# Decode attention with gated output: V read by whole batches through one ring of five 32 KB buffers

## The chip, the cores and the metric

One NeuronCore of a Trainium2 chip runs the whole kernel. The metric is the device time of one execution in microseconds. Engines are named as in the profile: PE (matmul), DVE, ACT, POOL, and SP, which only issues transfers here. A core has 16 DMA engines, and every large transfer is spread over all of them.

## The reference

One decode step for 8 sequences (batches): layer norm of `x`, attention over the last 2048 of 8192 cached positions with 32 query heads on 8 cached heads of 128, and a gated branch that multiplies the attention's result.

```python
# x: (8, 1, 512)   k_cache, v_cache: (8, 8, 8192, 128)   wq: (512, 4096)   wo: (4096, 512)
xn = layernorm(x)
W = min(4096, max(256, Sk // 4))                    # 2048
q = (xn @ wq).reshape(B, 1, 32, 128).transpose(0, 2, 1, 3)
k = repeat(k_cache[:, :, Sk - W:, :], 4, axis=1)    # 4 query heads share a cached head
v = repeat(v_cache[:, :, Sk - W:, :], 4, axis=1)
p = softmax(einsum("bhqd,bhkd->bhqk", q, k) * 128 ** -0.5)
s = (einsum("bhqk,bhkd->bhqd", p, v)).transpose(0, 2, 1, 3).reshape(B, 1, 4096) @ wo
h = sigmoid(xn @ w_gate) * (xn @ w_up)              # 512 x 1792 each
g = silu(h @ w_down)                                # 1792 x 512
return x + s * g
```

All inputs are bf16. The windows of K and of V are 33.5 MB each, `wq` and `wo` 4.2 MB each, the gated branch's weights 1.8 MB each: 81 MB are read.

## The kernel before

**Staging.** Everything is read once, all large reads by SP, in one order written out in `loads`: `wq`, K tiles 0 to 6, V tiles 0 and 1, K tile 7, V tiles 2 to 13, `w_gate` and `w_up`, V tiles 14 and 15, `w_down`, and `wo` in six pieces of 16, 8, 4, 2, 1 and 1 of its 32 rows per partition. There are two rings of buffers. `kring` has 3 of 32 KB per partition and takes `wq`, the K tiles and the three other weights; `vring` has 4 of 16 KB per partition and takes the V tiles. `issue_loads` puts the next load of the list on SP's queue once the tile that had its buffer before, 3 or 4 places back in the same ring, is in `released`, and it never passes one load over for a later one. In the program that comes out, SP's instruction waits for the reader of that older tile, so the loads behind it on SP wait too.

**Slots.** The loop over `t` writes the engines' orders by hand, one slot at a time. In slot `t` DVE turns an eighth of a K tile (`k_turn`, L464); four slots later PE multiplies it with the queries (`qk`, L479). K has 8 tiles of 8 slots, in two sets (`hb`) of four batches. At `EXP_AT[hb]` a set's softmax starts: `soft_exp` on ACT (L507), `soft_turn` on DVE (L527), `soft_spread` (PE L540, ACT L548), which brings the probabilities to the partitions of V, `soft_den` for the denominators. `soft_mask` (L561) multiplies them on DVE with the head masks `Hm`, so that one matmul can serve several heads whose rows stand in one contraction. From slot `PV_LAG` = 52 on PE takes V (`pv`, L609), beside the last K slots at first.

**V.** A V tile is half a batch: 4 of 8 cached heads, 32 runs of 64 positions by 4 heads on the 128 partitions, 16 KB each. `pv` makes 16 matmuls of a tile in 4 slots; each has a weight of 64 columns (4 heads x 4 position chunks x 4 query heads) and 512 columns of V (4 chunks x 128), and two of them fill the two halves of the output's 128 rows (`tile_position`). After the fourth slot ACT copies the sum to SBUF (L623). `pv_sum` (L635), once for four tiles and at the end for 2, 1 and 1, picks the diagonal blocks out of it with f32 matmuls against `Sel`, and DVE applies 1/denominator (L644).

**End.** `unit_in` (L355) and `unit_mid` make the gated branch's hidden layer once its weights are in, after V tile 13. After the last V tile `o_rows` (L657, DVE L664) brings the heads to the rows of `wo`, `unit_out` (L381) does `w_down`, and 64 matmuls (L723, 2 per row of `wo`) follow the pieces of `wo` as they land. DVE multiplies by the gate (L734), adds `x` (L736), and two transfers write the output.

The lines that tie loads to buffers:

```python
order, n = (v_order, VRING) if kind == 1 else (k_order, KRING)
at = order.index(x)
if at >= n and order[at - n] not in released:
    break
```

Of the kernel before, what the change touches and what calls it, by code (L numbers as in the profile page):

```python
# [10 lines left out]
def kernel(  # L11
# [13 lines left out]
    nc = tc.nc  # L25
# [18 lines left out]
    PP = P // GL  # L44
    CH = W // PP
    NQ = P // 32
    NJ = 4
    CC = CH // NJ
    NT = B * NG
# [11 lines left out]
    VSET = NT // HB  # L61
# [14 lines left out]
    NCH = 4  # L76
    KRING = 3
    VRING = 4
    CG = CH // NCH
# [17 lines left out]
    kring = ctx.enter_context(tc.tile_pool(name="kring", bufs=KRING))  # L97
    vring = ctx.enter_context(tc.tile_pool(name="vring", bufs=VRING))
# [19 lines left out]
    def k_tile(shape, name):  # L118
        return kring.tile(shape, bf16, name=name, tag="kring", align_bytes=ALIGN)

    def v_tile(shape, name):
        return vring.tile(shape, bf16, name=name, tag="vring", align_bytes=ALIGN)
# [8 lines left out]
    wq_sb = k_tile([P, KT, Hq * Dh], "wq_sb")  # L131
# [8 lines left out]
    def load_k(i):  # L140
        hb, kq = divmod(i, NK)
        t = k_tile([P, KC, Dh], "k_sb")
# [9 lines left out]
    def v_of(i):  # L152
        hb, n = divmod(i, VSET)
        gg, q = divmod(n, NQ)
        return NQ * hb + q, gg
# [15 lines left out]
    def load_gate_up():  # L171
        t = k_tile([P, 2, KT, F], "wgu_sb")
        for n, w in enumerate((B_w_gate, B_w_up)):
            load(t[:, n], w.rearrange("(p kt) n -> p kt n", kt=KT))
            wgu_sb.append(t[:, n])

    def load_down():
        t = k_tile([P, FT, D], "wd_sb")
# [6 lines left out]
    def load_wo():  # L185
        t = k_tile([P, KW, D], "wo_sb")
# [56 lines left out]
    x_f = ppool.tile([B, D], f32, name="x_f", tag="pp")  # L243
    nc.vector.tensor_copy(out=x_f[:], in_=x_bf[:])  # L244
    stats = work.tile([B, nc.vector.BN_STATS_DIM], f32, name="stats")
    nc.vector.bn_stats(out=stats[:], in_=x_f[:])
    mv = work.tile([B, nc.vector.BN_AGGR_DIM], f32, name="mv")
    nc.vector.bn_aggr(out=mv[:], in_=stats[:])
    eps_t = work.tile([B, 1], f32, name="eps_t")
    nc.vector.memset(eps_t[:], 1e-5)  # L250
    rstd = work.tile([B, 1], f32, name="rstd")
# [19 lines left out]
    for c in range(NCOL):  # L271
# [32 lines left out]
    Hm = consts.tile([P, GL], f32, name="Hm")  # L304
    nc.vector.tensor_reduce(
        out=Hm[:],
        in_=ident[:].rearrange("p (a gl) -> p gl a", gl=GL),
# [3 lines left out]

    spread = consts.tile([P, NG, 2, PP, GL], bf16, name="spread")
    nc.gpsimd.memset(spread[:].rearrange("p a b c d -> p (a b c d)").bitcast(f32), 0.0)
    for j in range(GL):
        for gg in range(NG):
            g = NG * gg + j // 2
            nc.gpsimd.tensor_copy(
                out=spread[:, gg, j % 2, :, j], in_=ident[:, 32 * g : 32 * g + PP]
            )

    w = NCH * GL * rep
    rows_of = ppool.tile([P, w], f32, name="rows_of", tag="pp")
    nc.vector.tensor_reduce(
        out=rows_of[:],
        in_=ident[:].rearrange("p (a m) -> p m a", m=w),
        axis=AX.X,
        op=ALU.add,
    )
    Sel = consts.tile([P, NCH, GL, rep], f32, name="Sel")
    nc.vector.tensor_copy(  # L330
        out=Sel[:], in_=rows_of[:].rearrange("p (g c r) -> p c g r", g=GL, c=NCH)
# [3 lines left out]
    pick = consts.tile([32 * NG, NE, P], bf16, name="pick")  # L335
    nc.gpsimd.memset(pick[:].rearrange("p e m -> p (e m)").bitcast(f32), 0.0)
    for gg in range(NG):
        rows = slice(32 * gg, 32 * (gg + 1))
        cols = slice(NE * GL * rep * gg, NE * GL * rep * (gg + 1))
        for e in range(NE):  # L340
            nc.gpsimd.tensor_copy(
                out=pick[rows, e, cols].rearrange("p (h d) -> p h d", d=NE)[:, :, e],
                in_=ident[rows, 32 * gg : 32 * gg + GL * rep],
            )
# [108 lines left out]
    o_sb = work.tile([32 * NG, B, Dh], bf16, name="o_sb")  # L453
    nc.vector.memzero(o_sb[:])
# [76 lines left out]
    def soft_spread(hb):  # L531

        pt = pt_of.pop(hb)[:].rearrange("p c (y m) -> p c y m", y=2)
        pc = ppool.tile([P, NG, NQ, CH, rep], bf16, name="pc_bf", tag="pp")
        for gg in range(NG):
            for ch in range(2):
                c = slice(CB * ch, CB * (ch + 1))
                pT_ps = psum_a.tile([P, CB, NQ, rep], f32, name="pT_ps", tag="acc_ps")
                for y in range(2):
                    nc.tensor.matmul(  # L540
                        pT_ps[:],
                        lhsT=spread[:, gg, y].rearrange("p k g -> p (k g)"),
# [4 lines left out]
                    )  # L547
                nc.scalar.copy(  # L548
                    out=pc[:, gg, :, c, :].rearrange("p q c r -> p c q r"),
# [4 lines left out]
    def soft_mask(hb, gg):  # L554

        pT_of[hb, gg] = work2.tile(
            [P, NQ * CG, GL, NCH * rep], bf16, name="pT_sb"
        )
        pc = pc_of[hb][:, gg].rearrange("p q (c e) r -> p (q c) (e r)", e=NCH)
        for gl in range(GL):  # L560
            nc.vector.tensor_scalar(  # L561
                out=pT_of[hb, gg][:, :, gl, :],
                in0=pc,
                scalar1=Hm[:, gl : gl + 1],
# [3 lines left out]

    GW = GL * rep

    def soft_den(hb):
# [8 lines left out]
        den_ps = psum1.tile([32 * NG, NQ], f32, name="den_ps", tag="misc")  # L580
        rden = small.tile([32 * NG, NQ], f32, name="rden")
        for gg in range(NG):
            rows = slice(32 * gg, 32 * gg + GW)
            nc.tensor.matmul(  # L584
                den_ps[rows, :],
                lhsT=HR[:, GL * gg : GL * (gg + 1)].rearrange("m h r -> m (h r)"),
                rhs=dq[:],
                start=True,
                stop=True,
                tile_position=(0, 32 * gg),  # L590
                skip_group_check=True,
            )
            nc.vector.reciprocal(out=rden[rows, :], in_=den_ps[rows, :])
        rden_of[hb] = rden

    def pv(t):


        i, j = divmod(t, NJ)
        b, gg = v_of(i)  # L600
        w = GL * rep * NCH
        if j == 0:
            acc_tiles[i] = psum_a.tile([P, NCH * Dh], f32, name="acc_ps", tag="acc_ps")
        q = b % NQ
        pT = pT_of[b // NQ, gg][:, CG * q : CG * (q + 1)].rearrange("p c g n -> p (c g n)")
        for n in range(CC // NCH):
            c = n % (P // w)
            ch = CC * j + NCH * n
            nc.tensor.matmul(  # L609
                acc_tiles[i][w * c : w * (c + 1), :],  # L610
                lhsT=pT[:, GL * rep * ch : GL * rep * ch + w],
                rhs=v_tiles[i][:, ch : ch + NCH, :].rearrange("p c d -> p (c d)"),
                start=(j == 0 and n < P // w),
                stop=(j == NJ - 1 and n >= CC // NCH - P // w),
                tile_position=(0, w * c),
                skip_group_check=True,
            )
        if j == NJ - 1:
            if i % NSUM == 0:
                acc_sbs[i // NSUM] = work.tile(  # L620
# [3 lines left out]
                out=acc_sbs[i // NSUM][:, i % NSUM], in_=acc_tiles.pop(i)[:]  # L624
            )

    def pv_sum(i, n):

        b, gg = v_of(i)
        q = b % NQ  # L630
        acc_sb = acc_sbs[i // NSUM][:, i % NSUM : i % NSUM + n]
        rows = slice(32 * gg, 32 * gg + GW)
        o_ps = psum1.tile([32 * NG, NSUM, Dh], f32, name="o_ps", tag="misc")
        for c in range(NCH):
            nc.tensor.matmul(  # L635
                o_ps[rows, :n, :],
                lhsT=Sel[:, c].rearrange("p g r -> p (g r)"),
# [3 lines left out]
                tile_position=(0, 32 * gg),  # L641
# [3 lines left out]
            out=o_sb[rows, b : b + n, :],  # L645
            in0=o_ps[rows, :n, :],
            in1=rden_of[b // NQ][rows, q : q + n].unsqueeze(2).to_broadcast([GW, n, Dh]),
# [21 lines left out]
    for t in range(PV_LAG + NSLOT):  # L669
# [3 lines left out]
        for hb in range(HB):  # L673
            if t == EXP_AT[hb]:
                soft_exp(hb)
            for gg in range(NG):
                if t == MASK_AT[hb, gg]:
                    soft_mask(hb, gg)
# [9 lines left out]
        if u >= NJ and u % NJ == 0:  # L688
            i = u // NJ - 1
            if i == NT - 2:  # L690
                pv_sum(i, 1)
# [80 lines left out]
```

## Time and profile before

| | |
|---|---|
| median of 3 runs | 197.33 us (197.1 to 197.42) |
| profiled execution, its own time | 197.29 us |
| its span in the profile | 195.5 us |
| PE busy | 102.9 us (53%), 750 instructions |
| DVE busy | 105.5 us (54%), 149 |
| ACT busy | 30.8 us (16%), 69 |
| SP's data queue (q1) | 81.01 MB, 97.0% of the 16 engines' span |
| mean granted PE clock | 0.903 |

The span runs from the first to the last instruction that the profiler recorded; the profiled execution took 1.8 us more than that. A chain of waits is followed back from the last instruction. In the tables of windows, each column gives an engine's busy microseconds and its instructions in brackets, then the granted clock, the share of the 16 DMA engines, and GB/s. Times in the text such as "at 173.1" are microseconds from the start of the span.

### The profile page before, as it was taken

The numbers are of one execution on the slowest core, as the hardware profiler recorded it, in microseconds if no ns is written. First come the engines' busy times: TensorE is split into PE (matmuls) and PEld (weight loads), VectorE is DVE, ScalarE is ACT, GpSimd is POOL, SyncE is SP. The second block draws the span as 40 slices with busy tenths as digits, with TensorE's granted clock in tenths as the row PEclk, the third lists the DMA queues.
The fourth block names the chain that finished last, engine by engine and source line by source line (L and its number), as shares of the span: only waits on it lengthen the run. The fifth ranks groups of instructions, "written<-read, shape, count | busy, mean of one in ns | idle before, by whom it ended". The sixth has DMA issues, their size and how long they took to land.

```text
span 195.5 us, 1888 instructions
## 1 busy us (share of the span) xinstructions
PE 102.9 (53%) x750; PEld 36.2 (19%) x750; DVE 105.5 (54%) x149; ACT 30.8 (16%) x69; POOL 4.6 (2%) x25
## 2 busy tenths in 40 slices
PE   0062014434323258403695989858944893577763
PEld 0020001101000012100121222322311131223551
DVE  0156499999899998899969726403100010040301
ACT  2025050000000084000011143511111114010100
POOL 8000000000000000000000000000000000000000
PEclk9999999999999999955588799988999798597999
DMA  7999999999999999999999999999999999999990
GB/s 276 423 476 429 436 429 429 429 429 421 429 429 429 429 429 429 389 432 463 429 419 432 436 422 429 427 429 429 429 429 432 429 431 425 431 429 432 425 390 30
DMA packets 5128, 81.14 MB, mean 415 GB/s; under 512 B 616, under 2 KB 896, under 8 KB 1152
## 3 DMA queue, kind: packets, MB, share of 16 engines
q1 hardware_dynamic: 5056, 81.01, 97.0%
q8 instruction: 6, 0.10, 0.2%
q10 hardware_dynamic: 64, 0.01, 0.0%
q14 instruction: 2, 0.02, 0.0%
HBM read 81.01 MB, written 0.01 MB: 414 GB/s over the span
## 4 chain that ended last, share of the span: by engine, by line
DMA 62%; DVE 23%; PE 10%; issue 1%; ACT 1%; SPq 0%; DVEq 0%
DMA k_sb<-in_A_k_cache_dram 31%; DMA v_sb<-in_A_v_cache_dram 22%; DVE k_sb L464 18%; DMA wo_sb<-in_A_wo_dram 10%; PE acc_ps L609 4%; DVE pt_bf L527 2%; PE s_ps L479 2%; PE pT_ps L540 2%; PE o_ps L635 2%; DVE mx L493 1%; SPq L116 0%; DVE qz_sb L434 0%; DVE o_sb L644 0%; PE den_ps L584 0%; DVE qT_sb L424 0%
## 5 line engine op out<-in xcount | busy, mean ns | idle before, releaser
L464 DVE STREAM_TRANSPOSE k_sb<-k_sb 128x1024 f32<-128x1024 f32 x64 | 73.7, 1210 | 6.7 <-DMA k_sb<-in_A_k_cache_dram 6.6
L479 PE MATMUL s_ps<-k_sb,qz_sb 128*32 128x512 bf16 x256 | 29.8, 565 | 54.2 <-DVE k_sb L464 48.4
L609 PE MATMUL acc_ps<-v_sb,pT_sb 128*64 128x512 bf16 x256 | 39.6, 443 | 10.7 <-DMA v_sb<-in_A_v_cache_dram 10.6
L644 DVE TENSOR_TENSOR o_sb<-o_ps,rden 16x512 bf16<-16x512 f32 (+2 forms) x6 | 3.0, 504 | 47.5 <-PE o_ps L635 47.5
L479 PEld LDWEIGHTS <-qz_sb 128*32 128x32 bf16 x256 | 8.5, 116 | 78.6 <-issue 55.3
L623 ACT COPY acc_sb<-acc_ps 128x512 f32<-128x512 f32 x16 | 9.4, 586 | 84.7 <-PE acc_ps L609 84.7
L609 PEld LDWEIGHTS <-pT_sb 128*64 128x64 bf16 x256 | 13.3, 120 | 31.5 <-DMA v_sb<-in_A_v_cache_dram 14.6
L635 PE MATMUL o_ps<-acc_sb,Sel 128*16 128x512 f32 (+2 forms) x48 | 15.9, 477 | 3.4 <-ACT acc_sb L623 3.4
L561 DVE TENSOR_SCALAR pT_sb<-pc_bf,Hm 128x1024 bf16<-128x1024 bf16 x16 | 6.6, 477 | 6.7 <-PE acc_ps L609 6.7
L507 ACT ACT_TABLE_LOAD x1 | 1.3, 1283 | 39.9 <-DVE nm L501 39.9
L635 PEld LDWEIGHTS o_ps<-acc_sb,Sel 128*16 128x16 f32 x48 | 4.5, 103 | 14.9 <-issue 7.7
L493 DVE TENSOR_REDUCE mx<-s_ps 128x1 f32<-128x512 f32 x8 | 5.3, 662 | 3.2 <-PE s_ps L479 3.2
L540 PE MATMUL pT_ps<-pt_bf,spread 128*128 128x512 bf16 x16 | 6.0, 501 | 1.3 <-DVE pt_bf L527 0.7
L267 PE MATMUL xnT_ps<-ident,xn_bf 8*128 8x8 bf16 x4 | 0.3, 174 | 11.6 <-DVE xn_bf L257 11.6
L436 ACT COPY qz_sb<-qT_sb 32x32 bf16<-32x32 bf16 x20 | 4.8, 241 | 8.2 <-DVE qT_sb L424 7.9
L355 PE MATMUL d_ps<-wgu_sb,xnT_sb 128*32 128x448 bf16 x32 | 3.0, 511 | 5.3 <-DMA wgu_sb<-in_B_w_up_dram 3.0
L723 PE MATMUL a_ps<-wo_sb,o_sb 128*32 128x256 bf16 x64 | 4.5, 273 | 2.0 <-DMA wo_sb<-in_A_wo_dram 2.0
L507 ACT ACTIVATE p_bf<-s_ps,nm 128x512 bf16<-128x512 f32 x8 | 5.4, 686 | 0.0
L244 DVE CAST x_f<-x_bf 8x512 f32<-8x512 bf16 x1 | 0.4, 415 | 9.2 <-DMA x_bf<-in_A_x_dram 9.2
L548 ACT CAST pc_bf<-pT_ps 128x512 bf16<-128x512 f32 x8 | 4.5, 587 | 5.0 <-DVE pt_bf L527 2.8
L527 DVE STREAM_TRANSPOSE pt_bf<-p_bf 128x512 bf16<-128x512 bf16 x8 | 4.9, 668 | 0.0
L723 PEld LDWEIGHTS <-o_sb 128*32 128x32 bf16 x64 | 3.5, 96 | 3.1 <-issue 3.0
(59 smaller groups left out, 39.4 us busy)
## 6 DMA issues: line engine op xcount, KB each, us to landing
k_sb<-in_A_k_cache_dram SPq DMA_DIRECT2D x8, 4096.0 KB, 19.3
v_sb<-in_A_v_cache_dram SPq DMA_DIRECT2D x16, 2048.0 KB, 15.7
wq_sb<-in_A_wq_dram SPq DMA_DIRECT2D x1, 3072.0 KB, 11.4
wo_sb<-in_A_wo_dram SPq DMA_DIRECT2D x1, 2048.0 KB
wgu_sb<-in_B_w_gate_dram SPq DMA_DIRECT2D x1, 1792.0 KB
wgu_sb<-in_B_w_up_dram SPq DMA_DIRECT2D x1, 1792.0 KB, 24.7
wd_sb<-in_B_w_down_dram SPq DMA_DIRECT2D x1, 1792.0 KB
wq_sb<-in_A_wq_dram SPq DMA_DIRECT2D x1, 1024.0 KB, 4.6
```

Of the source, the lines that this page charges most:

```text
L436: nc.scalar.copy(out=out, in_=in_)
L464: nc.vector.transpose(out=kw, in_=kw)
L479: nc.tensor.matmul(s_tiles[i][32 * g : 32 * (g + 1), :], lhsT=qz_sb[:, hb, h, 2 * a + e, :], rhs=kT[:, :, a, h, :, e], start=(n == 0), sto ...
L493: nc.vector.reduce_max(out=mx_of[hb][:, kq : kq + 1], in_=s_tiles[i][:], axis=AX.X)
L507: nc.scalar.activation(out=p_bf[:, :, kq], in_=s_tiles.pop(NK * hb + kq)[:].rearrange("p (o c j) -> p c j o", o=2, j=NC), func=AF.Exp, bia ...
L527: nc.vector.transpose(out=pt[:, w * n : w * (n + 1)], in_=p_bf[:, w * n : w * (n + 1)])
L540: nc.tensor.matmul(pT_ps[:], lhsT=spread[:, gg, y].rearrange("p k g -> p (k g)"), rhs=pt[:, c, y, :], start=(y == 0), stop=(y == 1), skip_ ...
L561: nc.vector.tensor_scalar(out=pT_of[hb, gg][:, :, gl, :], in0=pc, scalar1=Hm[:, gl : gl + 1], scalar2=None, op0=ALU.mult,)
L609: nc.tensor.matmul(acc_tiles[i][w * c : w * (c + 1), :], lhsT=pT[:, GL * rep * ch : GL * rep * ch + w], rhs=v_tiles[i][:, ch : ch + NCH, : ...
L623: nc.scalar.copy(out=acc_sbs[i // NSUM][:, i % NSUM], in_=acc_tiles.pop(i)[:])
L635: nc.tensor.matmul(o_ps[rows, :n, :], lhsT=Sel[:, c].rearrange("p g r -> p (g r)"), rhs=acc_sb[:, :, Dh * c : Dh * (c + 1)], start=(c == 0 ...
L723: nc.tensor.matmul(a_ps[32 * c : 32 * (c + 1), :], lhsT=o2_sb[:, k, :], rhs=wo_parts[k][:, DC * c : DC * (c + 1)], start=(k == 0), stop=(k ...
```

## The change

A V tile becomes a whole batch: 8 heads by 16 runs of 128 positions, 32 KB per partition, in one transfer; the last batch's comes in two halves of 16 KB. The two rings become one of five buffers of 32 KB (160 KB per partition, as the two rings had together), in the one order of `loads`, so a load waits for the tile five places back, whatever it holds. `w_gate` and `w_up` stand ahead of the last V tile. `pv` has 32 matmuls per tile in 8 slots, each with a weight of 128 columns (8 heads x 4 chunks x 4 query heads), no longer two side by side. Masks are made per batch, 8 of 512 elements per partition for batch `b` at `MASK_AT[b]`; those of batches 0 and 1 in the same slots as before, that of batch `b` later with the start of tile `b - 1`'s products (`pT_sb` still has two buffers). `pv_sum` comes for 4, 3 and 1 batches, and its outputs, the denominators and `pick` use 32 rows in place of two groups of 16. `wo` is cut into pieces of 12, 9, 5, 3, 2 and 1. Three small tiles of the layer norm share one, and `x` comes in two transfers instead of three.

```diff
-    NJ = 4
-    CC = CH // NJ
-    NT = B * NG
+    RUNS = P // Hkv
+    CV = W // RUNS
+    NCH = 4
+    CG = CV // NCH
+    NJ = 8
+    CGJ = CG // NJ
+    NT = B
...
-    MASK_AT = {}
-    for gg in range(NG):
-        MASK_AT[0, gg] = EXP_AT[0] + 9 + gg
-        MASK_AT[1, gg] = max(EXP_AT[1] + 6, PV_LAG + NJ * NQ * (gg + 1))
+    MASK_AT = {0: EXP_AT[0] + 9, 1: EXP_AT[0] + 10}
+    for b in range(2, NT):
+        MASK_AT[b] = PV_LAG + NJ * (b - 1)
...
-    KRING = 3
-    VRING = 4
+    RING = 5
...
-    for c0, c1 in ((0, 2), (2, 3), (3, 4)):
+    for c0, c1 in ((0, 2), (2, 4)):
         nc.scalar.dma_start(
...
-    def load_v(i):
-        b, gg = v_of(i)
-        t = v_tile([P, CH, Dh], "v_sb")
-        load(
-            t[:].rearrange("p c d -> p (c d)"),
-            A_v_cache[b, GL * gg : GL * (gg + 1), win0:Sk, :].rearrange(
-                "j (p c) d -> p j (c d)", c=CH
-            ),
-        )
-        v_tiles[i] = t
+    v_runs = A_v_cache[:, :, win0:Sk, :].rearrange(
+        "b h (k c) d -> b k h (c d)", c=CV
+    )
+
+    def load_v(b):
+        t = big([P, CV, Dh], "v_sb")
+        flat = t[:].rearrange("p c d -> p (c d)")
+        parts = 2 if b == NT - 1 else 1
+        n = CV * Dh // parts
+        for h in range(parts):
+            load(flat[:, n * h : n * (h + 1)], v_runs[b, :, :, n * h : n * (h + 1)])
+        v_tiles[b] = t
...
-            (0, 16),
-            (16, 24),
-            (24, 28),
-            (28, 30),
-            (30, 31),
+            (0, 12),
+            (12, 21),
+            (21, 26),
+            (26, 29),
+            (29, 31),
             (31, 32),
...
-    loads[-2:-2] = [(2, 0)]
+    loads[-1:-1] = [(2, 0)]
     loads = loads + [(2, 1), (2, 2)]
-    k_order = [(4, 0)] + [x for x in loads if x[0] != 1]
-    v_order = [x for x in loads if x[0] == 1]
+    order = [(4, 0)] + loads
...
-            order, n = (v_order, VRING) if kind == 1 else (k_order, KRING)
-            at = order.index(x)
-            if at >= n and order[at - n] not in released:
+            at = loads_done[0] + 1
+            if at >= RING and order[at - RING] not in released:
                 break
...
+    def soft_mask(b):
+
+        pT_of[b] = work2.tile([P, CG, Hkv, NCH * rep], bf16, name="pT_sb")
+        pc = pc_of[b // NQ][:, b % NQ].rearrange("p (c e) r -> p c (e r)", e=NCH)
+        for h in range(Hkv):
             nc.vector.tensor_scalar(
-                out=pT_of[hb, gg][:, :, gl, :],
+                out=pT_of[b][:, :, h, :],
                 in0=pc,
-                scalar1=Hm[:, gl : gl + 1],
+                scalar1=Hm[:, h : h + 1],
...
+    def pv(t):
+
+
+        b, j = divmod(t, NJ)
+        if j == 0:
+            acc_tiles[b] = psum_a.tile([P, NCH * Dh], f32, name="acc_ps", tag="acc_ps")
+        for cg in range(CGJ * j, CGJ * (j + 1)):
             nc.tensor.matmul(
+                acc_tiles[b][:],
+                lhsT=pT_of[b][:, cg].rearrange("p h n -> p (h n)"),
+                rhs=v_tiles[b][:, NCH * cg : NCH * (cg + 1), :].rearrange(
+                    "p c d -> p (c d)"
+                ),
+                start=(cg == 0),
+                stop=(cg == CG - 1),
                 skip_group_check=True,
             )
...
+        if u == NJ * NSUM:
+            pv_sum(0, NSUM)
+        elif u == NSLOT - NJ // 2:
+            pv_sum(NSUM, NT - NSUM - 1)
...
-        if u == NSLOT - 2 * NJ - 1:
+        if u == NSLOT - NJ - 1:
             unit_in(wgu_sb[0])
             unit_in(wgu_sb[1])
             released.add((2, 0))
             issue_loads()
-        if u == NSLOT - 2 * NJ:
+        if u == NSLOT - NJ:
             unit_mid()
```

More of the change, by code (lines that the diff above doesn't have):

```diff
@@ L60 @@
     SET = NK * KTS
-    VSET = NT // HB
     QK_LAG = 4
@@ L116, in load, with big @@
         q.dma_start(out=dst, in_=src)
[L118 to L122, printed above, removed]
+    def big(shape, name):
+        return ring.tile(shape, bf16, name=name, tag="ring", align_bytes=ALIGN)
     x_bf = work.tile([B, D], bf16, name="x_bf")
-    for c0, c1 in ((0, 2), (2, 3), (3, 4)):
+    for c0, c1 in ((0, 2), (2, 4)):
         nc.scalar.dma_start(
@@ L141, in load_k @@
         hb, kq = divmod(i, NK)
-        t = k_tile([P, KC, Dh], "k_sb")
+        t = big([P, KC, Dh], "k_sb")
         k0 = win0 + NC * KC * kq
@@ L302 @@
     )
-    Hm = consts.tile([P, GL], f32, name="Hm")
+    Hm = consts.tile([P, Hkv], f32, name="Hm")
     nc.vector.tensor_reduce(
         out=Hm[:],
-        in_=ident[:].rearrange("p (a gl) -> p gl a", gl=GL),
+        in_=ident[:].rearrange("p (a h) -> p h a", h=Hkv),
         axis=AX.X,
@@ L310 @@
     )
[L312 to L316, printed above, removed]
+    spread = consts.tile([P, 2, 2, P], bf16, name="spread")
+    nc.gpsimd.memset(spread[:].rearrange("p a b c -> p (a b c)").bitcast(f32), 0.0)
+    for o in range(2):
+        for y in range(2):
             nc.gpsimd.tensor_copy(
-                out=spread[:, gg, j % 2, :, j], in_=ident[:, 32 * g : 32 * g + PP]
-            )
[L321 to L329, printed above, removed]
+                out=spread[:, o, y].rearrange("p (k g s) -> p s g k", g=NQ, s=2)[:, y],
+                in_=ident[:].rearrange("p (g k o) -> p o g k", k=RUNS, o=2)[:, o],
+            )
+    Sel = consts.tile([P, NCH, Hkv, rep], f32, name="Sel")
     nc.vector.tensor_copy(
-        out=Sel[:], in_=rows_of[:].rearrange("p (g c r) -> p c g r", g=GL, c=NCH)
+        out=Sel[:], in_=ident[:].rearrange("p (h c r) -> p c h r", c=NCH, r=rep)
     )
     NE = P // Hq
-    pick = consts.tile([32 * NG, NE, P], bf16, name="pick")
+    pick = consts.tile([Hq, NE, P], bf16, name="pick")
     nc.gpsimd.memset(pick[:].rearrange("p e m -> p (e m)").bitcast(f32), 0.0)
[L337 to L344, printed above, removed]
+    for e in range(NE):
+        nc.gpsimd.tensor_copy(
+            out=pick[:, e, :].rearrange("p (h d) -> p h d", d=NE)[:, :, e],
+            in_=ident[:Hq, :Hq],
+        )
     FQ = F // 4
@@ L452 @@
     acc_sbs = {}
-    o_sb = work.tile([32 * NG, B, Dh], bf16, name="o_sb")
-    nc.vector.memzero(o_sb[:])
+    o_sb = work.tile([Hq, B, Dh], bf16, name="o_sb")
     def k_turn(t):
@@ L533, in soft_spread @@
         pt = pt_of.pop(hb)[:].rearrange("p c (y m) -> p c y m", y=2)
-        pc = ppool.tile([P, NG, NQ, CH, rep], bf16, name="pc_bf", tag="pp")
-        for gg in range(NG):
+        pc = ppool.tile([P, NQ, CV, rep], bf16, name="pc_bf", tag="pp")
+        for o in range(2):
             for ch in range(2):
@@ L547, in soft_spread @@
                     )
+                cv = slice(CH * o + CB * ch, CH * o + CB * (ch + 1))
                 nc.scalar.copy(
-                    out=pc[:, gg, :, c, :].rearrange("p q c r -> p c q r"),
+                    out=pc[:, :, cv, :].rearrange("p q c r -> p c q r"),
                     in_=pT_ps[:],
@@ L579, in soft_den @@
         )
[L580 to L593, printed above, removed]
+        den_ps = psum1.tile([Hq, NQ], f32, name="den_ps", tag="misc")
+        rden = small.tile([Hq, NQ], f32, name="rden")
+        nc.tensor.matmul(
+            den_ps[:],
+            lhsT=HR[:].rearrange("m h r -> m (h r)"),
+            rhs=dq[:],
+            start=True,
+            stop=True,
+        )
+        nc.vector.reciprocal(out=rden[:], in_=den_ps[:])
         rden_of[hb] = rden
     def pv(t):
-        i, j = divmod(t, NJ)
-        b, gg = v_of(i)
-        w = GL * rep * NCH
+        b, j = divmod(t, NJ)
         if j == 0:
[L603 to L615, printed above, removed]
+            acc_tiles[b] = psum_a.tile([P, NCH * Dh], f32, name="acc_ps", tag="acc_ps")
+        for cg in range(CGJ * j, CGJ * (j + 1)):
+            nc.tensor.matmul(
+                acc_tiles[b][:],
[5 more added lines that the diff above has]
+                stop=(cg == CG - 1),
                 skip_group_check=True,
@@ L618, in pv @@
         if j == NJ - 1:
-            if i % NSUM == 0:
-                acc_sbs[i // NSUM] = work.tile(
+            if b % NSUM == 0:
+                acc_sbs[b // NSUM] = work.tile(
                     [P, NSUM, NCH * Dh], f32, name="acc_sb"
@@ L623, in pv, with pv_sum @@
             nc.scalar.copy(
[L624 removed]
+                out=acc_sbs[b // NSUM][:, b % NSUM], in_=acc_tiles.pop(b)[:]
             )
[L627 to L629 removed]
+    def pv_sum(b, n):
         q = b % NQ
[L631 to L633 removed]
+        acc_sb = acc_sbs[b // NSUM][:, b % NSUM : b % NSUM + n]
+        o_ps = psum1.tile([Hq, NSUM, Dh], f32, name="o_ps", tag="misc")
         for c in range(NCH):
             nc.tensor.matmul(
[L636 to L637 removed]
+                o_ps[:, :n, :],
+                lhsT=Sel[:, c].rearrange("p h r -> p (h r)"),
                 rhs=acc_sb[:, :, Dh * c : Dh * (c + 1)],
@@ L644, in pv_sum @@
         nc.vector.tensor_tensor(
-            out=o_sb[rows, b : b + n, :],
-            in0=o_ps[rows, :n, :],
-            in1=rden_of[b // NQ][rows, q : q + n].unsqueeze(2).to_broadcast([GW, n, Dh]),
+            out=o_sb[:, b : b + n, :],
+            in0=o_ps[:, :n, :],
+            in1=rden_of[b // NQ][:, q : q + n].unsqueeze(2).to_broadcast([Hq, n, Dh]),
             op=ALU.mult,
@@ L675 @@
                 soft_exp(hb)
-            for gg in range(NG):
-                if t == MASK_AT[hb, gg]:
-                    soft_mask(hb, gg)
+        for b in range(NT):
+            if t == MASK_AT[b]:
+                soft_mask(b)
         if t < KSLOT:
```

49 lines of the change are left out of this document (14 added, 35 removed).

## The prediction

> **What bounds the kernel now.** I read the slices of the page first, then the chain that ended last, then the groups, and last the timelines of PE and DVE near the end. The slices, and one window of the V stage:
>
> ```profile
> GB/s 276 423 476 429 436 429 429 429 429 421 429 429 429 429 429 429 389 432 463 429 419 432 436 422 429 427 429 429 429 429 432 429 431 425 431 429 432 425 390 30
> DMA packets 5128, 81.14 MB, mean 415 GB/s; under 512 B 616, under 2 KB 896, under 8 KB 1152
> ```
> ```profile
> 110.00:160.00 50.00, 38.27 (x226) 12.32 (x224) 10.62 (x24) 11.32 (x23) 0.00 (x0) 0.93 1.00 428
> ```
>
> After the first slice the transfers run at about 429 GB/s to the end, with K (slices 4 to 17) and with V (18 on) alike; the single dips to 389 and 419 stand beside 432 and 463 and are packets booked in the neighbouring slice. The packet records confirm it: each of the 16 DMA engines starts a packet as the one before ends. 81.0 MB at 429 GB/s are 189 us of a 195.5 us span: the kernel is as long as its reads, plus a start of 2 us and an end of 3.4 us. The chain in order of time shows that end:
>
> ```profile
> 128.32 16.83 DMA v_sb<-in_A_v_cache_dram
> ...
> 147.14 25.99 DMA v_sb<-in_A_v_cache_dram
> 173.13 0.02 issue
> 173.15 18.96 DMA wo_sb<-in_A_wo_dram
> 192.11 0.04 issue
> 192.15 0.30 PE a_ps L723 x2
> 192.45 0.02 issue
> 192.47 0.42 DVE prod L734
> 192.90 0.02 issue
> 192.92 0.28 DVE y_bf L736
> ```
>
> The last piece of wo lands at 192.11; everything else is done by then. So the change can act in three ways only: on the time a byte takes, on an issue that comes too late to keep the engines fed, or on compute that is not ready for the last wo piece.
>
> ```profile
> L464 DVE STREAM_TRANSPOSE k_sb<-k_sb 128x1024 f32<-128x1024 f32 x64 | 73.7, 1210 | 6.7 <-DMA k_sb<-in_A_k_cache_dram 6.6
> L609 PE MATMUL acc_ps<-v_sb,pT_sb 128*64 128x512 bf16 x256 | 39.6, 443 | 10.7 <-DMA v_sb<-in_A_v_cache_dram 10.6
> L561 DVE TENSOR_SCALAR pT_sb<-pc_bf,Hm 128x1024 bf16<-128x1024 bf16 x16 | 6.6, 477 | 6.7 <-PE acc_ps L609 6.7
> ```
>
> V's matmuls wait for V's transfers (10.6 us), K's transposes for K's (6.6): the engines run after the data.
>
> **Part by part. 1, packets.** The bytes and their order are unchanged; V goes from 16 transfers with 16 KB runs to 7 with 32 KB runs and two halves with 16 KB. K is read in 32 KB runs already, so both prices are in the trace: one engine needs 1.210 us from packet to packet of 32 KB, 0.6074 us of 16 KB, and about 6 ns for the semaphore write of a transfer. Per engine 4 MB of V are 16 x 0.6074 + 2 x 0.006 = 9.73 us now and 8 x 1.210 + 0.006 = 9.69 us then; landings 4.86 us apart for 2 MB and 9.68 us for 4 MB say the same. Seven tiles save 7 x 0.043 = 0.30 us. wo is cut otherwise (12, 9, 5, 3, 2, 1 of 32 for 16, 8, 4, 2, 1, 1): six pieces, as many packets, the same last piece, so nothing. One x transfer fewer is 8 packets of 18 ns beside wq, which is the later: nothing.
>
> [...]
>
> **2, one ring of five.** A load now needs the tile five places back. From a tile's landing to the moment when the load that replaces it must be queued lie four tiles, some 39 us. Dating the releases by the trace: k0 is free at 35 (SP issues k3 at 34.98), needed for k5 by 60; k3 at 64.6, needed for k7 by 89; k5 at 92, for v2 by 109; v0 at about 106, for v4 by 127; k7 at 116, for v5 by 137. Every margin is above 15 us, so SP's waits stay ahead of the engines, though the ring is in one order. No cost; without that cover an issue late by some us would cost as many.
>
> **3, V's products.** Before, two 64-column matmuls ran side by side: 16 took 1.92 us at full clock, 0.22 us a pair, and at the half clock 3.56:
>
> ```profile
> 173.18 1.92 PE L609 MATMUL acc_ps<-v_sb,pT_sb 128*64 128x512 bf16 x16 [0.76 <-DMA v_sb<-in_A_v_cache_dram]
> 178.03 3.56 PE L609 MATMUL acc_ps<-v_sb,pT_sb 128*64 128x512 bf16 x16 [1.21 <-DMA v_sb<-in_A_v_cache_dram]
> 123.34 1.08 PE L540 MATMUL pT_ps<-pt_bf,spread 128*128 128x512 bf16 x4 [0.40 <-ACT pc_bf L548]
> ```
>
> Now 256 matmuls of 128 columns stand one by one. The L540 row gives their spacing, (1.08 - 0.38) / 3 = 0.23 us, and PE's own starts 0.216; I take 0.22, so a tile of 32 needs 7.1 us, under the 9.7 that its read takes, and 13.7 at the half clock. Added PE time 256 x 0.11 = 28 us, all beside transfers. Taken out: half of the f32 sums of L635 (15.9 us to about 8) and 8 evictions of 0.59 us.
>
> **4, masks.** 64 of 512 elements for 16 of 1024 (0.40 us apart). Between a half (0.20) and a whole (0.40) I take 0.28: 18 us for 6.6. Those of batches 0 and 1 lie among K's transposes: 16 x 0.28 - 3.3 = 1.2 us late, less 0.5 for one den round trip instead of two; DVE waits 1.95 us for k7 at 101.5, so it hides. Batch 2's mask waits for V tile 0's last product and stands ahead of k7's last four transposes: PE's slots there are 0.33 + 0.86 = 1.2 us, as long as DVE's, and the second softmax comes some 1.5 us later than at 114.4. V tile 2, the first behind it, lands at 121; with the half clock for one window and L540's eight products it is done at 131.5, tile 3 at 138.6, the first sum at 142.2, tile 4 at 149.3, and tile 5 lands at 150: caught up.
>
> **5, the end.** The first half of v7 lands at 172.9, the second at 177.7. At full clock: 16 products 3.5 us to 176.4, the sum over three batches 8 x 0.32 = 2.6 to 179.0, second half to 182.6, eviction to 183.3, last sum to 184.4, o_sb 184.7, pick 185.3, cast 1.29 to 186.6, b_ps beside it; wo's 64 matmuls (3.5 us) from 186.8 could end at 190.3. Before they began at 187.12, at a landing. wo lands until 191.8, so 1.5 us are spare, and one half-clock window of 3.4 us, the length in the trace, costs 1.7. It just hides.
>
> **Sum.** 192.11 - 0.30 = 191.8, then 3.4 us as now: span 195.2; the profiled execution took 197.29, 1.79 more than its span: 196.99. The median is 0.04 higher: 197.03. A measurement of this kernel can tell about 0.2% (0.39 us) from no change; this is 0.15%.
>
> **Rivals.** *A DMA engine that loses twice.* Each of the six 16 KB packets of q8 (instructions) holds one engine up by 0.9 us and its next packet by 0.5; the 8 KB ones of q14 by 0.3 and 0.5. After the first of each at 46 to 48 us the 16 landings of a transfer lie 1.6 us apart instead of 0.3, and stay so: each fetch hits another engine, so the slowest carries one. DVE has some 40 instructions more and PE as many as now. One more fetch, or another sequence, on an engine already late costs 0.8 to 1.4 us: 197.8 to 198.4. For it: half the engines are already hit. Against: eight fetches have not met so far. 0.14.
>
> *PE late at the end, so slower.* The granted clock fell to 0.5 at 178.1 after a window with 1.5 us of work in 3.4, and at 82.6, 106.5, 130.4, 150.8, 164.5 likewise. In the new order PE is idle 3 us before v7's first half, so one cold window is likely; a second, in b_ps and wo's products, makes 3.4 - 1.5 = 1.9 us at most: 197.5 to 198.9. It decides from the point where wo's products start later than 188.3. Against: from 172.9 to 182.6 PE now has work without a pause. 0.09. [...]
>
> [...] 0.02.
>
> *Fewer transfers gain more*: if each of the 7 dropped transfers stood in the line with its own start-up, the 1.1 us from the first issue (0.74) to the first packet (1.80), 197 - 8 = 189. The back-to-back packets are against it. 0.01. [...]
>
> *The change as described, ending on the read* has the remaining 0.74. Its own range is 196.6 to 197.4: the 0.30 may be 0.1 to 0.6, since which engine is hit last moves the end by up to the 0.3 us that landings differ before any fetch, and the three runs before spread over 0.3. About 0.32 of it lies below 196.94, 0.40 within 0.2%, 0.02 above. With the rivals: faster 0.33, same 0.40, slower 0.27. The range goes up to 198.1, into the first two rivals, and down to 196.5.
>
> **What would show it.** Right: GB/s at 429 to the last slice, last wo landing near 191.8, the chain still ending in wo; 32 V matmuls in about 7 us; masks near 0.28 us each; SP issues long ahead of use. Wrong: a slice under 420 in the V stage (a late issue, or pitch), landings of one transfer 2.5 us apart (a double fetch), or PE's wo products running on after the last landing without waiting.

## The result and the profile after

The changed kernel takes 285.49 us (median of 4 runs, 282.46 to 289.29), the kernel before 197.36 (4 runs, 197.1 to 197.42): ratio 1.442, 95% interval [1.429, 1.455]. The forecast was 197.0, within 196.5 to 198.1. The profiled execution is the longest of the four, 289.29 us with a span of 287.5, so differences of two per cent or less are not read from it.

The slices of the page, and the window that answers the one of before, in the V stage (its last figure is GB/s, the one before it the share of the DMA engines):

```profile
GB/s 311 419 438 438 438 434 435 438 438 438 438 223 217 205 374 292 205 214 214 219 214 217 219 211 191 205 210 214 221 210 220 204 237 341 203 219 217 346 339 22
DMA packets 4104, 81.13 MB, mean 282 GB/s; under 512 B 480, under 2 KB 640, under 8 KB 1024
```
```profile
110.00:160.00 50.00, 22.28 (x112) 6.42 (x111) 17.69 (x34) 3.86 (x10) 0.00 (x0) 0.70 1.02 213
```

K's seven tiles still run at 438 GB/s. From the twelfth slice on, where V begins, it is about 214, half of it, at a DMA share of 1.02: the 16 engines are not waiting for an issue, each packet simply takes longer. The packet records say the same: 32 KB of K take 1.213 us, 32 KB of V mostly 2.37 to 2.55 (median 2.50). In K tile 7 (374 and 292) and the weights (341, 346, 339) the rate rises again.

The end of the chain (steps below 0.6 us left out), and V's products and the masks among the groups:

```profile
217.50 9.71 PE acc_ps L576 x32
228.04 9.57 another core or an unknown queue
237.96 3.84 another core or an unknown queue
242.14 9.02 another core or an unknown queue
251.18 32.59 DMA wo_sb<-in_A_wo_dram
283.81 0.63 PE a_ps L684 x6
```
```profile
L576 PE MATMUL acc_ps<-v_sb,pT_sb 128*128 128x512 bf16 x256 | 76.5, 458 | 76.7 <-DMA v_sb<-in_A_v_cache_dram 76.7
L540 DVE TENSOR_SCALAR pT_sb<-pc_bf,Hm 128x512 bf16<-128x512 bf16 x64 | 17.4, 343 | 50.1 <-PE acc_ps L576 50.1
```

The chain still ends in the last piece of `wo`, now at 283.8 instead of 192.1. PE waits 76.7 us for V, 10.6 before. The place of the loss is V's reading: 33.5 MB at 213 instead of 429 GB/s are 157 us instead of 78, 79 of the 92 us between the two profiled executions. The other 13 us, by subtraction, lie among K tile 7 and the weights, whose packets run in between: the 16 landings of one V transfer are 7.5 us apart (1.6 before), so fast and slow transfers are in flight together. If each engine's packets are followed by their starts and ends, K tile 7's first ones, from 99 us on, took mostly 2.2 to 2.4 us, the next mostly 1.3 to 1.5, and from 104 us on 1.21, as one engine after another left V tile 0.

### The profile page after: what moved, and what is told of

Read it like the earlier page. It is cut to its first block, busy times and chain, and to the rows that moved or that the text cites. A ratio compares the mean times of both kernels' runs of the same rounds, so it can differ in the third digit from the quotient of the medians.

```text
span 287.5 us, 1840 instructions
## 1 busy us (share of the span) xinstructions
PE 130.0 (45%) x722; PEld 47.2 (16%) x722; DVE 113.4 (39%) x190; ACT 26.1 (9%) x61; POOL 4.1 (1%) x17
## 4 chain that ended last, share of the span: by engine, by line
another core or an unknown queue 31%; DMA 28%; PE 21%; DVE 16%; SPq 1%; issue 1%; ACT 0%; ACTq 0%
DMA k_sb<-in_A_k_cache_dram 17%; PE acc_ps L576 16%; DVE k_sb L444 13%; DMA wo_sb<-in_A_wo_dram 11%; PE pT_ps L520 1%; SPq L114 1%; DVE pT_sb L540 1%; PE s_ps L459 1%; PE o_ps L601 1%; DVE pt_bf L507 1%; DVE mx L473 1%; PE a_ps L684 0%; ACT acc_sb L591 0%; ACT pc_bf L529 0%
## 5 line engine op out<-in xcount | busy, mean ns | idle before, releaser
L576 PE MATMUL acc_ps<-v_sb,pT_sb 128*128 128x512 bf16 x256 | 76.5, 458 | 76.7 <-DMA v_sb<-in_A_v_cache_dram 76.7
L576 PEld LDWEIGHTS <-pT_sb 128*128 128x128 bf16 x256 | 27.1, 112 | 121.3 <-issue 64.2
L540 DVE TENSOR_SCALAR pT_sb<-pc_bf,Hm 128x512 bf16<-128x512 bf16 x64 | 17.4, 343 | 50.1 <-PE acc_ps L576 50.1
L591 ACT COPY acc_sb<-acc_ps 128x512 f32<-128x512 f32 x8 | 4.7, 586 | 174.5 <-PE acc_ps L576 174.5
L609 DVE TENSOR_TENSOR o_sb<-o_ps,rden 32x512 bf16<-32x512 f32 (+2 forms) x3 | 1.5, 501 | 23.4 <-PE o_ps L601 23.4
L352 DVE TENSOR_TENSOR h_sb<-sig,d_ps 128x448 bf16<-128x448 f32 x1 | 0.6, 622 | 22.8 <-PE d_ps L336 22.8
L601 PE MATMUL o_ps<-acc_sb,Sel 128*32 128x512 f32 (+2 forms) x24 | 7.5, 454 | 1.4 <-ACT acc_sb L591 1.4
L386 PE MATMUL q_ps<-wq_sb,xnT_sb 128*32 128x512 bf16 x32 | 3.8, 627 | 1.8 <-DMA wq_sb<-in_A_wq_dram 1.8
```

The costliest lines, as they stand in the source:

```text
L540: nc.vector.tensor_scalar(out=pT_of[b][:, :, h, :], in0=pc, scalar1=Hm[:, h : h + 1], scalar2=None, op0=ALU.mult,)
L576: nc.tensor.matmul(acc_tiles[b][:], lhsT=pT_of[b][:, cg].rearrange("p h n -> p (h n)"), rhs=v_tiles[b][:, NCH * cg : NCH * (cg + 1), :].re ...
L591: nc.scalar.copy(out=acc_sbs[b // NSUM][:, b % NSUM], in_=acc_tiles.pop(b)[:])
L601: nc.tensor.matmul(o_ps[:, :n, :], lhsT=Sel[:, c].rearrange("p h r -> p (h r)"), rhs=acc_sb[:, :, Dh * c : Dh * (c + 1)], start=(c == 0), ...
```

## The experiments

In the tables of windows below the last three columns are the granted PE clock, the DMA share and GB/s.

**Is it the transfer, and what of it?** Three kernels change V's transfers alone, or K's alone in the kernel before. v32x4_16k takes the changed kernel with V in the shape of before:

```diff
-        parts = 2 if b == NT - 1 else 1
-        n = CV * Dh // parts
-        for h in range(parts):
-            load(flat[:, n * h : n * (h + 1)], v_runs[b, :, :, n * h : n * (h + 1)])
+        n = CH * Dh
+        for h in range(2):
+            load(
+                flat[:, n * h : n * (h + 1)],
+                A_v_cache[b, GL * h : GL * (h + 1), win0:Sk, :].rearrange(
+                    "j (p c) d -> p j (c d)", c=CH
+                ),
+            )
```

> The changed kernel with V read in the old shape: per batch two transfers of 32 runs of 16 KB by 4 heads, into the two halves of the 32 KB buffer. The bytes are the same, but they lie in other places than the products expect, so the sums over V are other sums; every instruction and its time stay. Theory A, the shape (the first axis of V's source has 16 entries instead of 32, and the shares of the 16 DMA engines then collide on the way into SBUF): V at 429 GB/s again, 197 to 198 us, all of the loss gone. Theory B, HBM addresses (8 heads 2 MiB apart, streams 32 KB apart): the old addresses are back, the same 197 to 198. Theory C, something else of the change (ring of five, 128-column products, masks): it stays at 280 or so, or keeps a part.

v32x4_32k has one transfer of 32 rows by 4 heads, with runs of 32 KB and heads 2 MiB apart:

```diff
+        rows = A_v_cache[b, :GL, Sk - 2 * W : Sk, :].rearrange(
+            "j (p c) d -> p j (c d)", c=CV
+        )
         for h in range(parts):
-            load(flat[:, n * h : n * (h + 1)], v_runs[b, :, :, n * h : n * (h + 1)])
+            load(flat[:, n * h : n * (h + 1)], rows[:, :, n * h : n * (h + 1)])
```

> The changed kernel with V read in one transfer per batch of 32 rows by 4 heads with 32 KB runs: rows 32 KB apart over the last 4096 positions of heads 0 to 3. Other data of V, as many bytes. Theory A (shape): 32 first, so full rate, and the 0.3 us that 32 KB packets save against v32x4_16k: 197.0. Theory B (addresses): the streams are still 32 KB apart and the heads 2 MiB, so half rate as in the changed kernel: about 285. Theory D (runs of 32 KB for V): half rate, about 285.

k16x8 leaves V alone and reads K in the kernel before as 16 rows by 8 runs of 32 KB:

> The kernel before with K's tiles in the shape of the new V: 16 rows (2 batches by 8 heads, 2 MiB apart) by 8 runs of 32 KB, where it reads 32 rows by 4 runs now. The tiles hold the same bytes of K in sum, but other ones than the scores expect. Theory A (shape): K falls to about 214 GB/s, 33.5 MB take 157 us instead of 78, some 276 us in all, V untouched. Theory B (addresses): K's rows are 2 MiB apart and its runs 32 KB as before: 197.3, unchanged. Theory D (runs of 32 KB for V): unchanged.

Measured: v32x4_16k 198.28 us (ratio 1.0045 [1.0026, 1.0064]), v32x4_32k 197.50 (1.0016 [0.9991, 1.0041]), k16x8 278.44 (one run). V was read at 427 and 424 GB/s in the first two (140 to 160 us), K at 210 in the third (20 to 80 us). So the loss lies in the transfer, not in the ring, the products or the masks, which v32x4_32k has in full; and not in runs of 32 KB or heads 2 MiB apart, since v32x4_32k has both. It goes with the split, to K as well. The slices of k16x8, where K is slow and V is not:

```profile
GB/s 320 364 227 227 223 194 190 227 227 223 194 193 223 223 223 185 208 223 223 223 204 213 424 298 218 192 374 424 433 430 426 436 426 429 433 429 429 436 413 124
```

**Eight rows.** v8x16 puts the heads first, in the changed kernel: `"b h (k c) d -> b h k (c d)"`.

> The changed kernel with the axes of V's source exchanged: 8 heads first, then 16 runs. The rows of a tile stand in another order than the masks expect. [...] Theory B (addresses): 8 streams 2 MiB apart, nothing that sets a number; 285 or slower.

450.34 us, near an estimate of some 430: half of the engines, with packets twice as long, make V's 78 us four times as long (197 + 3 x 78). With V alone (150 to 228 us) eight packets are in flight, so not every large transfer is spread over all 16 engines; each takes 1.9 to 2.6 us with a median of 2.46, and from 140 to 160 us V is read at 108 GB/s at a DMA share of 0.50, a quarter of the 429 of before (the window below also holds a stretch with `w_gate` and `w_up`):

```profile
150.00:350.00 200.00, 51.28 (x195) 18.62 (x200) 14.90 (x45) 7.17 (x16) 0.00 (x0) 0.62 0.59 118
```

With half of the engines idle a packet is as slow (2.46 us) as with all 16 (2.50), so the loss isn't a total rate that all engines share. While K tile 7 ran beside V tile 0 (82 to 107 us), all 16 packets took about 3.0 to 3.7 us, K's too.

**The ring alone.** ring5 is the kernel before with one ring of five, a pair of V tiles to a buffer.

> The kernel before with one ring of five 32 KB buffers; a V buffer takes two of its tiles, each read as before by one transfer of 32 runs of 16 KB by 4 heads. Products and masks are those of before. If the ring is harmless, as the prediction has it (margins of 15 us): 197.3, within 0.2%. If loads in one order come late: slower by the lateness, seen as a slice under 420 GB/s.

197.25 us, ratio 0.9997 [0.9987, 1.0007]: the ring costs nothing.

**Addresses.** v16x8_odd reads 16 rows by 8 runs at pitches that are no powers of two:

```diff
+    ODD = RUNS * 9 * 144
+    v_odd = A_v_cache.rearrange("b h s d -> b (h s) d")[:, :ODD, :].rearrange(
+        "b (r j c) d -> b r j (c d)", r=RUNS, j=9
+    )[:, :, :Hkv, : CV * Dh]
```

> The changed kernel with V's 16 rows by 8 runs of 32 KB taken at pitches of 36,864 bytes between runs and 331,776 bytes between rows, no power of two (other data of V than the batch needs). If the addresses at powers of two are what is slow: about 197 to 199. If it is the shape of 16 by 8 whatever the addresses: 282 to 290.

292.78 us, with V at 212 GB/s from 140 to 160 us: pitches at powers of two are not the cause.

**The side of SBUF, first try.** v16x4_pair splits each batch in two transfers of 16 runs by 4 heads, into partitions 0 to 63 and 64 to 127; v32x2_pair does the same with 32 rows by 2 heads.

```diff
-            load(flat[:, n * h : n * (h + 1)], v_runs[b, :, :, n * h : n * (h + 1)])
+            for a in range(2):
+                load(
+                    flat[64 * a : 64 * (a + 1), n * h : n * (h + 1)],
+                    v_runs[b, :, 4 * a : 4 * (a + 1), n * h : n * (h + 1)],
+                )
...
```

(The lines left out change the order of heads in two constants and move one sum.)

> The changed kernel with V in two transfers per batch, each of 16 runs by 4 heads (32 KB packets, still 16 rows first) into partitions 0 to 63 and 64 to 127, so that an engine holds 4 neighbouring partitions of a transfer and not 8; the order of heads in the mask and spread constants follows, and the sum of the first three of the last batches' accumulators is taken before the last V tile's products. Theory P (the eight neighbouring partitions that one engine writes are what is slow): packets of 1.21 us again and 197.0 us (196.8 to 197.6). Theory S (a first axis of 16 is what is slow, whatever the partitions): packets of about 2.4 us and 280 to 290 us.

> Beside the pair of 16 by 4: the changed kernel with V as two transfers of 32 rows by 2 heads into 64 partitions each (other data of V than the batch needs, runs of 32 KB). Both theories P and S give full rate, about 198. A third (64 partitions at a time have only half of the ways into SBUF) gives 270 to 290 here, and then a slow pair of 16 by 4 would say nothing between P and S.

282.72 us (ratio 1.434 [1.431, 1.438]) and 284.57. The second is the one that tells: with 32 rows first, which ran at full rate into 128 partitions (424 GB/s in v32x4_32k from 140 to 160 us), it is half rate into 64 (211 in the same window). A first axis of 16 is not needed for the loss, and of the expectations only the third, half rate into 64 partitions at a time, stands.

**The place in SBUF.** v64_where has the same transfers at two places:

```diff
+        lo = 32 if b % 4 in (1, 2) else 0
...
+        if b < 4:
+            src = (wide[:, 0:2, :], wide[:, 2:4, :])
+        else:
+            src = (v_runs[b, :, 0:4, :], v_runs[b, :, 4:8, :])
+        for s in src:
+            load(flat[lo : lo + 64, :], s)
...
```

> The changed kernel with each batch's V as two transfers of 2 MB into 64 partitions, the second over the first (so half of the tile is never loaded; GpSimd fills it with zeros): batches 0 and 3 as 32 rows by 2 heads into partitions 0 to 63, batches 1 and 2 the same into 32 to 95, batches 4 and 7 as 16 runs by 4 heads into 0 to 63, batches 5 and 6 the same into 32 to 95. [...] Theory R (64 partitions at a time are half rate wherever they lie): 2.45 us in all eight. Theory S (a first axis of 16 is slow by itself): 5 and 6 at 2.45 us though 1 and 2 are at 1.21. [...]

265.98 us. Windows over the transfers of batch 0, of 1 and 2, of 3, of 4, of 5 and 6, and of 7 (the first column of figures is GpSimd's filling):

```profile
80.50:103.50 23.00, 13.70 (x3) 0.54 0.84 186
119.00:138.50 19.50, 11.57 (x2) 0.70 0.91 350
139.00:161.00 22.00, 18.12 (x3) 0.73 0.91 191
162.00:183.00 21.00, 8.68 (x2) 0.62 0.89 197
184.00:209.00 25.00, 6.92 (x1) 0.99 0.78 316
219.00:240.00 21.00, 0.00 (x0) 0.66 0.86 186
```

The windows hold some idle time, as the second transfer waits for the first, and the second one begins with the end of batch 1. The packets are clearer; the median of the 128 of each batch:

| batch | 0 | 3 | 1 | 2 | 4 | 7 | 5 | 6 |
|---|---|---|---|---|---|---|---|---|
| rows by heads | 32x2 | 32x2 | 32x2 | 32x2 | 16x4 | 16x4 | 16x4 | 16x4 |
| partitions | 0-63 | 0-63 | 32-95 | 32-95 | 0-63 | 0-63 | 32-95 | 32-95 |
| us | 2.56 | 2.56 | 1.21 | 1.21 | 2.53 | 2.53 | 1.36 | 1.22 |

The same transfer of 64 partitions is at full rate in one place (1.21 to 1.36 us a packet) and at half rate (2.53 to 2.56) 32 partitions further down, with either first axis. R and S fall: here the place decides, not the number of partitions and not the first axis alone. Why the two places differ no run here shows.

What that makes of 16 runs by 8 heads, into all 128 partitions, is a guess of mine. Which engine writes what isn't in the records. But eight rows kept eight packets in flight (v8x16), and reads of 4 and of 12 rows left three groups of 4, 8 and 4 engines (shift4, below), as if each engine took whole rows. With 16 rows that would be eight neighbouring partitions for each engine, and engines in step would write partitions 0, 8, 16 and so on at one moment. If some of them hinder each other then, putting the engines out of step should shorten the packets.

**Does the engines' step matter?** Two early runs put the engines out of step ahead of V tile 0 by reads of 4 rows and of 12 rows into a tile that nothing reads, with a ring of four. Each row has 4 runs of 32 KB in shift4 and 2 in shift2; the lines are shift4's:

```diff
+        load(spare[: 4 * 4, :], rows[:4, :4, :])
+        load(spare[16 : 16 + 12 * 4, :], rows[:, :4, :])
```

> The changed kernel, V in its 16 by 8 shape, with two reads put ahead of V tile 0 that nothing uses: one of 4 rows by 4 runs of 32 KB and one of 12 rows by 4, into a buffer of their own (the ring has four buffers to make room). They put the DMA engines out of step: some get 8 packets more, some 4, some none. [...] Theory E: the 16 by 8 shape is slow whatever the engines' step (its addresses, its descriptors): 285 us and the 5 to 10 us of the reads, 290 to 295.

> As shift4, but 4 rows by 2 runs and 12 rows by 2: the difference is 2 packets, a quarter of a share. [...] Theory E: 285 us and 3 to 5, as without them.

290.85 and 302.88 us, no gain in the whole time, and I took the guess of engines in step for refuted. That was too quick: shift4's slices (7.2 us each) show a gain in the middle of V.

```profile
GB/s 309 422 435 431 435 435 433 436 435 435 435 236 224 213 218 218 218 209 204 345 354 381 342 213 223 222 222 213 220 241 194 202 302 200 222 220 230 387 187 12
```

From 137 to 166 us V was read at 355 GB/s, with packets of 1.35 us in the median; before and after, at 2.4 to 2.6. What speaks against the guess is V tile 0, right behind the extra reads: its landings lie in three groups (4 near 100, 8 near 109, 4 near 119 us), so the engines were apart, and its packets still took some 2.4 us. Why it gained nothing is not shown. shift2 has no such stretch in V.

After v64_where the question came back. The next run meant to put 8 engines one transfer behind, after K tile 7, with a read of 8 rows by 4 runs:

> The run v16x4_pair with a ring of four buffers, batch 7 in two transfers instead of four, and one more read of 1 MB ahead of batch 1's V (8 rows by 4 runs of 32 KB into a tile that nothing reads), so that 8 of the 16 engines run four packets, one transfer, behind the others from batch 1 on. [...] If the step of the engines does not matter, or if they fall back into step: packets of 2.45 us and 280 to 290 us.

292.49 us; but that read, whose rows were contiguous, was shared by all 16 engines: its 16 landings came from 116.34 us on, 13 of them within 0.9 us. It put no engine behind, but it serves as a control: with a ring of four and an extra read, V still ran at 214 GB/s from 134 to 156 us and 211 from 156 to 196, as in the changed kernel. The last two use the 4 and 12 rows of shift4 instead, ahead of batch 1:

> v16x4_offset again, with another extra read ahead of batch 1's V, since the read of 8 by 4 was shared by all 16 engines (16 landings, from 116.34 us on) and put none behind: here 4 rows by 4 runs and 12 rows by 4 runs of 32 KB into a tile that nothing reads, which in shift4 left three groups of engines (4, 8, 4) each four packets apart. [...] If the step does not matter or is not kept: about 2.45 us and 285 to 295 us.

> The same two reads ahead of batch 1's V with V as in the changed kernel, one transfer of 16 by 8 per batch (ring of four; the masks in the order of the pair run, so with other weights than the batch needs). [...]

283.83 and 278.60 us: the time is near what was expected if the step does not matter, but the packets are not. The changed kernel, then v16x8_offset2 in the same three windows (the fourth line is the stage after, with `w_gate`, `w_up` and the last V tile):

```profile
84.00:98.00 14.00, 2.52 (x20) 0.60 (x19) 14.00 (x22) 0.00 (x0) 0.00 (x0) 0.50 1.03 217
134.00:156.00 22.00, 12.80 (x60) 3.58 (x60) 4.45 (x14) 3.28 (x9) 0.00 (x0) 0.73 1.02 214
156.00:196.00 40.00, 23.38 (x82) 8.66 (x83) 6.64 (x22) 3.32 (x6) 0.00 (x0) 0.80 1.00 211
```
```profile
84.00:100.00 16.00, 2.52 (x20) 0.60 (x19) 15.74 (x23) 0.00 (x0) 0.00 (x0) 0.50 1.06 222
134.00:156.00 22.00, 11.02 (x59) 3.40 (x60) 0.63 (x1) 0.00 (x0) 0.00 (x0) 0.69 1.00 348
156.00:196.00 40.00, 27.51 (x114) 10.79 (x115) 12.65 (x43) 7.37 (x16) 0.00 (x0) 0.99 1.00 306
205.00:250.00 45.00, 17.40 (x82) 6.44 (x81) 4.24 (x11) 3.00 (x4) 0.00 (x0) 0.74 0.99 199
```

Before the offset V runs as in the changed kernel (222). Behind it the same transfers, into the same partitions, run at 348 and 306 GB/s instead of 214 and 211; the median packet of 134 to 156 us takes 1.37 us instead of 2.53 (16 by 4 in v16x4_offset2: 1.31 and 361 GB/s, but 258 from 156 to 196). From 205 us on, with other transfers between, it is 199 again. The transfer and its partitions being the same, only the engines' step is left to explain the difference. How it acts is not shown, and the account is not complete: the rate stays short of 429, and V tile 0 of shift4 does not fit. The two windows moved 7.7 and 12.2 MB, for which 214 and 211 GB/s would need 36 and 58 us in place of 22 and 40: 32 us won. Of that some 10, by estimate, went into the 2 MB of extra reads at the slow rate. At V tile 5's landing this run was 20 us ahead of the changed kernel (197.8 against 217.5), at `wo`'s last landing 12.5 (271.6 against 284.1); what took the rest was not followed up.

**What is left of the change at full rate.** v32x4_32k was 0.2% above the kernel before, which its interval can't tell from no change, and v32x4_16k 0.5%, with runs from 197.0 to 198.9. The end of v32x4_32k (a run of 198.36 us), in its chain:

```profile
179.40 2.70 PE o_ps L604 x8
182.10 3.57 PE acc_ps L579 x16
...
188.36 1.64 PE b_ps L365 x28
189.99 3.51 PE a_ps L687 x64
193.50 0.02 issue
```

`wo`'s 64 products begin at 189.99 and run without a wait to 193.50: PE is late. v32k_early_sum was meant to test it, but ran v32x4_32k again:

> v32x4_32k once more for its page beside the other runs: 197.0 if PE runs at full clock after the first half of the last V tile, 198.4 if at half clock, as the ten runs before lay between 197.0 and 198.8.

It gave 197.94 us, within its range, with `wo`'s products from 189.53 on and again no wait. v32x4_early then has the edit:

```diff
-        elif u == NSLOT - NJ // 2:
+        elif u == NSLOT - NJ:
             pv_sum(NSUM, NT - NSUM - 1)
```

> The run v32x4_32k (the changed kernel with V as 32 rows by 4 heads, 32 KB runs, other data than the batch needs) with the sum of batches 4 to 6 taken before the last V tile's products instead of in their middle. There TensorE ran without a wait from 173 to 193.5 us and the last wo products started at 190.0, 1.4 us late; 2.7 us of sum moved ahead of the cold products should bring them back to waiting for wo's last landing: 197.0 us (196.9 to 197.3) in every run, where v32x4_32k had 197.0 to 198.8. If the lateness has another cause: 197.5 as before.

197.06 us (12 runs, 196.85 to 197.48), ratio 0.9987 [0.9978, 0.9997], and the chain ends on the read again (a step of 0.04 us left out):

```profile
168.16 23.56 DMA wo_sb<-in_A_wo_dram
191.76 0.63 PE a_ps L687 x6
```

That is 0.13% under the kernel before, but with V's data read in an order that the computation can't use; a transfer of whole batches with 32 KB runs, the right heads and full rate was not found.

## Why the prediction was wrong

**Part 1 failed**, in one term: "K is read in 32 KB runs already, so both prices are in the trace". The price of a packet was carried from K to V by its size alone. K's rows are 32 by 4 and V's became 16 by 8; no transfer of 16 rows over 128 partitions was in the trace of before. The term 8 x 1.210 us measured 8 x 2.5 (the median of 702 packets), 213 GB/s instead of 429. As the trace didn't show the shape, the term needed two ends; the far one, half the rate, is 78 us more for V, some 275 us in all.

**The only case with a slower byte had the wrong reason.** The 0.02 among the chances is for the pitch of 2 MiB between V's heads, with V at three quarters of the rate, 223 us. No run shows that term. In its place they showed the full rate at that pitch with 32 rows by 4 (430 GB/s in v32x4_32k from 110 to 160 us), half of it without powers of two (212 in v16x8_odd), and half with the changed split (213). Pitch was the only ground considered; how the split places a transfer's rows on the partitions was not looked at.

**Part 2 held**: ring5 is unchanged, and SP's issues stayed ahead in the changed kernel (DMA share 1.02).

**Parts 3 and 4 held in what they cost.** Masks: 17.4 us for 64, 0.27 each (0.28 forecast). A tile's 32 products take 7.07 us at the full clock in v32x4_32k (7.1 forecast). One date inside part 4 was off: with V at full rate the second softmax's exponentials begin at 122.88 there, 7.4 us later than before (115.48), not 1.5, and PE first waits for V again at 158, not at 150. It still hid.

**Part 5 failed too**, though it only shows with V at full rate: in v32x4_32k `wo`'s products began at 189.99, not at 186.8. The term is v7's first half, 3.5 us in the sum and 6.4 in the run (173.02 to 179.40, at a mean granted clock of 0.56); the sum over three batches (2.70), the second half (3.57) and the 4.3 us from there to `wo` came out as forecast. The cold window was priced at 1.7 us against 1.5 spare and measured 2.9. So the rival "PE late at the end" was what a change with a good transfer would have met in part of its runs: 5 of the 10 lie in its range of 197.5 to 198.9, the profiled one at 198.36. A chance of 0.09 was too little for it. v32x4_early confirms the place: with the sum moved ahead, the end is the read.

**The saving of 0.30 us** from longer packets is only roughly confirmed at full rate: against 192.11 before, `wo`'s last landing is 0.24 us earlier in v32x4_32k's profile and 0.06 in v32x4_early's, whose median is 0.22 us under that of before.

**What was to show it wrong** did: "a slice under 420 in the V stage". Of the two reasons named beside it, a late issue and the pitch, neither was the cause.

## What to carry to other kernels

The time of a packet is not set by its size alone: ask, for every transfer, by what split and into which partitions it writes. Of packets of 32 KB, a first axis of 32 over all 128 partitions (K, 1.21 us) or 64 partitions from 32 to 95 (1.21 to 1.36) had the full rate here; 16 by 8 over 128 (2.50), or the partitions 0 to 63 alone (2.53 to 2.56), ran at half, and 8 by 16, with eight packets of 2.46 us in flight, at a quarter. When a trial run shifts only one stage, read the rate of that stage, not the whole time: shift4 showed its effect there. A change of a transfer's layout that keeps bytes and run lengths can still change its rate, and the trace prices only the shapes that it holds.

## What was not expected of the hardware

- One slow transfer slows what is in flight beside it: K tile 7's packets of 1.21 us took up to 2.4 us beside V tile 0 in 16 by 8, and 3.0 to 3.7 beside 8 by 16. By what path it does so is not shown.
- The loss does not wear off: the 16 landings of a V transfer were 7.5 us apart, yet all 702 packets of 32 KB that began between 116 and 225 us took 2.34 us or more. Only runs with extra reads of four packets on some engines had stretches of 1.3 to 1.4 us.
- 64 partitions from 32 on are twice as fast a target as 64 from 0 (mostly 1.21 to 1.36 us a packet against 2.53 to 2.56).
